# Holding one batch's v loads and moving their casts in a fused linear-attention and MLP kernel

## The chip, the cores and the metric

The kernel runs on one core of a Trainium2 chip. The metric is the device time of one launch in microseconds (us); lower is better. A core has TensorE (PE in the profile, its weight loads PEld), VectorE (DVE), ScalarE (ACT), GpSimd (POOL) and SyncE (SP), each with an instruction stream of its own that is executed in order, and 16 DMA engines, which the queues of SP, ACT and POOL share.

## The reference

Inputs q, k, v are [8 batches, 8 heads, 576 tokens, 64]; the MLP has a gain of 512, w_ch1 of 512x2048 and w_ch2 of 2048x512, all float32. The inputs that matter are computed so:

```python
q_s = exp(q - max(q, -1));  q_s /= sum(q_s, -1) + 1e-9
k_s = exp(k - max(k, 2));   k_s /= sum(k_s, 2) + 1e-9
kv  = einsum('bhsd,bhse->bhde', k_s, v)
att = einsum('bhsd,bhde->bhse', q_s, kv)
x   = att.transpose(0, 2, 1, 3).reshape(8, 576, 512)
xn  = (x - mean(x)) / sqrt(var(x) + 1e-6) * g_ln
out = x + relu(xn @ w_ch1) @ w_ch2
```

## The kernel before, in words

**Chunks.** The MLP runs over nine chunks of 512 tokens. Chunks 0 to 7 are the first 512 tokens of batches 0 to 7, in four blocks t = 0..3 of 128; chunk 8 is the 64 remaining tokens of all eight batches. Chunk c's MLP runs on TensorE while the attention of batch c+1 (and the softmax of batch c+2) is woven between its matmuls. From the second half of chunk 1's first product on, both products are done in seven block products instead of eight, at the price of sums and differences of blocks: sum_x (L244, tile tq, on POOL for most chunks) for the inputs of the first product, sum_h (L561, tile hs, on DVE) for those of the second.

**Order.** Everything stands inside a manual schedule: each engine executes its instructions in the order in which the Python code emits them. run() (L820) walks the list of the main matmul steps of one chunk, adds up their weights, and before each step emits every side step whose position is not above the sum so far. A matmul of the block products weighs 0.5. Chunk 1 has 116 such units: 32 of a plain first product (ph, L505), 28 of the seven-product form (L733, tiles bx, bb, bc), and 56 of the second product (L588, tiles ba, bb, bc, be). Chunks 2 and later have 56 + 56. A position in the diff is thus a place in every engine's stream. Semaphores are derived from the tiles that instructions read and write.

**Buffers.** Tiles come from pools with a fixed number of buffers for each tag, and a new tile takes a buffer when an earlier tile of the tag has been used for the last time. The tag that matters is "ot" of the pool outp, with 4 buffers (L66). It holds the float32 output tiles of 128x512 (y_quarter L594, y_out L518), which are given up when their store to memory is complete, and, for batch 3 alone, the two bf16 halves of v (L145), which are given up when cast_v (L135) has copied them into vm. PSUM tiles "m" have 6 banks (mm_ps, L70); "a" has 2 (att_ps).

**Chunk 1's second product** (mm2_fast L666, lines 706 to 717) allocates four output tiles. Blocks t = 0 and 1 get theirs inside the fifth product (positions 93 and 94.5), where their first column half is written; the second half and the store (L605, issued by POOL) come in the seventh product (about 108.5 and 110). Blocks t = 2 and 3 get theirs in the seventh product (about 111.5 and 113), and have both halves written there.

**Side steps of chunk 1** (second_side, L867) that the change or the prediction speaks of: load_v(3) at 10.1, two loads of v as float32 to bf16 on POOL's queue and two small ones of the remaining tokens (vr, L158); kv_pairs(2) at 40 and the four x_fast(2, t) (L434: a scalar_tensor_tensor from PSUM tile po to x with its sum, L449, and xn, L429); the transposes xn_T(2, 0, 2) at 57.5 and xn_T(2, 2, 2) at 73 by the SP queue (L267); the four sum_x(2, i) on POOL from 95 to 105, which read both transposes; cast_v(3, 0) and cast_v(3, 1) at 101 and 102. POOL therefore has the sums of batch 2 in its stream ahead of all four stores of chunk 1.

**First stage of chunk 2** (attn_fast(3), L851; prep_fast; mm1_fast L736): reduce_q(3, 0, 2) at 4 and reduce_q(3, 2, 2) at 12, their reciprocal at 22, kv_pairs(3) at 24, which reads vm and vr of batch 3, and load_batch(4) at 1, whose loads of q and k are held back by a one-element memset on DVE (L1063). In mm1_fast each pair of groups g, g+1 takes six PSUM banks (x, c, b for each); the product order is 1, 5, 6, 2, 7, 3, 4, and between them stand the ACT copies (L757, L761), the DVE sums add_5 (L764) and out_22 (L767) with its max (L772).

Of the kernel before, what the change touches and what calls it, by code (L numbers as in the profile page):

```python
# [20 lines left out]
def kernel(  # L21
# [16 lines left out]
    nc = tc.nc  # L38
# [66 lines left out]
    def main_src(x, b, h0, hn):  # L105
        return x[b, h0 : h0 + hn, 0:SM, :].rearrange("h (p t) d -> p h (t d)", t=T)
# [28 lines left out]
    def cast_v(b, j):  # L135
        hs = slice(4 * j, 4 * j + 4)
        nc.vector.tensor_copy(
            out=vm[:, b % 2, :, hs, 0:D].rearrange("p t h d -> p h t d"), in_=vts[b][j]
        )

    def load_v(b):

        if b in CAST:
            if b == 3:
                vts[b] = [outp.tile([P, 4, T, D], BF16, tag="ot", name="vt") for _ in range(2)]  # L145
            else:
                vt = mlp.tile([P, H, T, D], BF16, tag=("tq", "hs")[b - 1], name="vt", bufs=1)
                vts[b] = [vt[:, 0:4], vt[:, 4:8]]
            for j, vt in enumerate(vts[b]):
                nc.gpsimd.dma_start(  # L150
                    vt.rearrange("p h t d -> p h (t d)"), main_src(v, b, 4 * j, 4)
                )
        src = v[b, :, 0:SM, :].rearrange("h (p t) d -> p t h d", t=T)
        for t in range(0 if b in CAST else T):
            nc.gpsimd.dma_start(vm[:, b % 2, t, :, 0:D], src[:, t])
        for half in range(2):
            hs = slice(4 * half, 4 * half + 4)
            nc.gpsimd.dma_start(  # L158
                vr[SR * half : SR * half + SR, b % 2, hs, 0:D],
                v[b, hs, SM:S, :].transpose([1, 0, 2]),  # L160
            )
# [54 lines left out]
    def reduce_q(c, t, tn=1):  # L216
        ts = slice(t, t + tn)
        nc.vector.reduce_sum(eqs[c][1][:, ts], eqs[c][0][:, ts], axis=AX.X)  # L218
# [128 lines left out]
    def kv_pairs(b, ts=range(T + 1)):  # L347

        par = b % 2
        if 0 in ts:  # L350
            kvbox["p"] = att_ps.tile([P, NP, P], FP32, tag="a", name="pkv")
        pkv = kvbox["p"]
        for j in range(NP):
            for t in ts:
                for half, ps in enumerate(halves):
                    h = 2 * j + half
                    if t < T:
                        lhsT, rhs = eks[b][:, t, h], vm[:, par, t, h]
                    else:
                        lhsT, rhs = ekr[:, par, h % 4], vr[:, par, h]  # L360
                    nc.tensor.matmul(  # L361
                        pkv[ps, j, 0:VW], lhsT, rhs, start=(t == 0 and j == 0),
                        stop=(t == T), skip_group_check=True,
                    )
        if T in ts:
            rzk = sml.tile([P, NP], FP32, tag="rzk", name="rzk")
            nc.vector.reciprocal(rzk, pkv[:, :, D])
            for half, ps in enumerate(halves):
                nc.vector.tensor_mul(
                    kv_sb[ps, b, :, ps], pkv[ps, :, 0:D], rzk[ps].to_broadcast([64, NP, D])  # L370
                )
# [42 lines left out]
    def square_sum(c, t):  # L414
        x, _, _, mv = xs[c]
        if c:
            nc.scalar.activation(  # L417
                scrap, x[:, t], AF.Square, bias=mv[:, t, 0:1], scale=-float(DM),
                accum_out=mv[:, t, 1:2],
            )  # L420
        else:
            nc.scalar.activation(
                scrap, x[:, t], AF.Square, bias=mv[:, t, 0:1], accum_out=mv[:, t, 1:2]
            )

    def xn_out(c, t):

        x, _, xn, mv = xs[c]
        nc.vector.tensor_scalar(  # L429
            out=xn[:, t], in0=x[:, t], scalar1=float(DM), scalar2=mv[:, t, 0:1],  # L430
            op0=ALU.mult, op1=ALU.subtract,
        )

    def x_fast(c, t):  # L434

        x, st, _, mv = xs[c]
        if c == C9:
            for half in range(2):
                nc.vector.scalar_tensor_tensor(
                    x[:, t].rearrange("p (i two d) -> p i two d", two=2, d=D)[:, :, half],  # L440
                    in0=pobox[c, t][half][:, t % 2], scalar=1.0,
                    in1=eqs[c][2][:, t].rearrange("p (i two) -> p i two", two=2)[:, :, half]
                    .to_broadcast([P, NP, D]),
                    op0=ALU.mult, op1=ALU.mult, accum_out=st[:, t, half : half + 1],
                )
            nc.vector.tensor_add(mv[:, t, 0:1], st[:, t, 0:1], st[:, t, 1:2])
            xn_out(c, t)
            return
        nc.vector.scalar_tensor_tensor(  # L449
            x[:, t].rearrange("p (h d) -> p h d", h=H),  # L450
            in0=pobox[c, t].rearrange("p (h d) -> p h d", h=H), scalar=1.0,
            in1=eqs[c][2][:, t].to_broadcast([P, H, D]), op0=ALU.mult, op1=ALU.mult,
            accum_out=mv[:, t, 0:1] if c else st[:, t, 0:1],
        )
        if c:
            xn_out(c, t)
# [359 lines left out]
    def spread(fns, a, b):  # L816
        n = len(fns)
        return [(a + (b - a) * i / n, fn) for i, fn in enumerate(fns)]
# [29 lines left out]
    def recip_q(c):  # L848
        nc.vector.reciprocal(eqs[c][2], eqs[c][1])

    def attn_fast(c):  # L851

        s = [(4 + 4 * t, lambda t=t: reduce_q(3, t, 2)) for t in (0, 2)] if c == 3 else []
        kv, new, ps, squares, ts, rstd = (
            (24, 40, ((48, 53), (57, 59), (65, 67), (73, 75)), (66, 74, 87, 91), (61, 78), 95)
            if c == 3 else
            (3, 10, ((13, 24), (48, 53), (57, 59), (65, 67)), (60, 66, 74, 87), (55, 70), 92)
        )
        s += [(22 if c == 3 else 2, lambda: recip_q(c)), (kv, lambda: kv_pairs(c)), (new, lambda: start_x(c))]
        for t, (p0, p1) in enumerate(ps):  # L860
            s += spread([lambda t=t, i=i: po_mm(c, t, i) for i in range(NP)], p0, p1)
            s += [(p1, lambda t=t: x_fast(c, t)), (squares[t], lambda t=t: square_sum(c, t))]
        s += [(ts[0], lambda: xn_T(c, 0, 2)), (ts[1], lambda: xn_T(c, 2, 2)), (rstd, lambda: rstd_op(c))]
        s += [((84, 100 if c == C9 - 1 else 88, 92, 101)[i], lambda i=i: sum_x(c, i)) for i in range(4)]
        return s

    def second_side():  # L867

        s = [(p, lambda i=i: quarter_w2(i, 6, 2)) for i, p in enumerate((19, 19.1, 33.9, 66))]
        s += [(6, lambda: xn_pT(1, 3, nc.scalar))]  # L870
        s += [((3, 3.1, 7.5, 7.6)[t], lambda t=t: exp_qt(2, t)) for t in range(T)] + [(7.7, lambda: eq_T(2))]
        s += [(40, lambda: square_sum(1, 2)), (63, lambda: square_sum(1, 3)), (67, lambda: rstd_op(1))]
        s += [(10, lambda: load_batch(3, (2,), eqTs[2][0:1, T - 1, NP - 1, 0:4])), (37, lambda: load_batch(3, (0,)))]
        s += [(p, lambda j=j: cast_v(2, j)) for j, p in enumerate((23, 32.2))]
        s += [(at, lambda i=i: sum_x(1, i)) for i, at in enumerate((9.1, 9.2, 31.5, 36))]
        s += [(10.1, lambda: load_v(3))]
        s += [(101 + j, lambda j=j: cast_v(3, j)) for j in range(2)]
        s += [(9 + 2 * t, lambda t=t: reduce_q(2, t, 2)) for t in (0, 2)]
        s += [(36, lambda: recip_q(2))]
        s += [(18, lambda: exp_k(2, 0, 4)), (28.5, lambda: exp_k(2, 2, 4)), (33, lambda: prep_kvrem(2))]  # L880
        s += [(40, lambda: kv_pairs(2))]
        s += [(40, lambda: start_x(2))]
        for t, (p0, p1) in enumerate(((47, 49), (51, 54), (57, 61), (65, 69))):
            s += spread([lambda t=t, i=i: po_mm(2, t, i) for i in range(NP)], p0, p1)
            s += [(p1, lambda t=t: x_fast(2, t)), ((69, 78, 84, 90)[t], lambda t=t: square_sum(2, t))]
        s += [(57.5, lambda: xn_T(2, 0, 2)), (73, lambda: xn_T(2, 2, 2)), (96, lambda: rstd_op(2))]
        s += [(81, lambda: exp_q(3, 0, 4)), (86, lambda: exp_q(3, 2, 4)), (90, lambda: eq_T(3))]
        s += [(102, lambda: exp_k(3, 0, 4)), (109, lambda: exp_k(3, 2, 4)), (111, lambda: prep_kvrem(3))]
        s += spread([lambda i=i: sum_x(2, i) for i in range(4)], 95, 108)
        return s  # L890
# [283 lines left out]
```

## Time and profile before

| | us |
|---|---|
| Median of 3 runs | 264.73 (264.06 to 266.44) |
| Span of the profiled execution, first to last instruction | 262.9 |
| PE busy in it | 255.6 (97%) |
| DVE busy | 223.4 (85%) |
| ACT busy | 176.8 (67%) |
| POOL busy | 94.2 (36%) |
| TensorE's mean granted clock | 0.998 |

Of the profiled execution the span alone is recorded; the median lies 1.83 us above that span, for what comes before the first and after the last instruction. Times in the views are counted from the start of the span. In a timeline each row is: start, duration, engine, line, operation, output <- input with partitions x elements and type, the count of instructions merged, and in brackets the idle time of the engine ahead of it with what ended it. In a table of stages each row is a stretch, its length, then for PE, PEld, DVE, ACT and POOL the busy time with the count, the granted clock, the mean number of busy DMA transfers per engine, and GB/s.

### The profile page before, as it was taken

To read this page: it belongs to the slowest core of one execution; us is meant where nothing else is said; L and a number is where in the kernel's file an instruction comes from. 1 tells how busy PE (TensorE), PEld (TensorE's weight loads), DVE (VectorE), ACT (ScalarE), POOL (GpSimd) and SP (SyncE) were. 2 spreads that over 40 slices of the span, in tenths; PEclk is the share of its full clock that TensorE was granted. 3 is DMA by queue.
4 is the path that set the end of the run, shared out by engine and by line. 5 is a ranking of instruction groups with operands and counts; after the bars stand their busy time and mean duration, and the time that the engine had idled before them with its cause. 6 is when DMAs were issued, how large, how long until landed. Compare 5 with 4: busy or idle time off the path is not lost.

```text
span 262.9 us, 6770 instructions
## 1 busy us (share of the span) xinstructions
PE 255.6 (97%) x2656; PEld 220.1 (84%) x2659; DVE 223.4 (85%) x504; ACT 176.8 (67%) x348; POOL 94.2 (36%) x148
## 2 busy tenths in 40 slices
PE   8999999999999999999999999999999999999993
PEld 6789755788878998899899988988898888888882
DVE  6768996989998999799889988998898979977872
ACT  4647780997976886689578957894789277537400
POOL 4953228414039404930781088009100800030000
PEclk9999999999999999999999999999999999999999
DMA  6999999998999995899489938994905323221014
GB/s 204 252 202 207 358 215 269 282 188 260 187 151 341 232 119 58 266 278 111 100 251 280 140 82 270 261 167 100 271 11 107 113 102 44 42 110 52 0 41 120
DMA packets 82504, 45.00 MB, mean 171 GB/s; under 512 B 58084, under 2 KB 79080, under 8 KB 82472
## 3 DMA queue, kind: packets, MB, share of 16 engines
q0 software_dynamic: 32464, 21.76, 45.3%
q1 hardware_dynamic: 49424, 22.29, 40.1%
q10 hardware_dynamic: 584, 0.53, 0.6%
q8 instruction: 20, 0.33, 0.5%
q14 instruction: 12, 0.10, 0.1%
HBM read 36.70 MB, written 9.44 MB: 175 GB/s over the span
## 4 chain that ended last, share of the span: by engine, by line
PE 89%; DMA 4%; POOL 2%; DVE 2%; issue 1%; ACT 0%; POOLq 0%
PE ba L588 20%; PE bx L733 19%; PE bb L733 10%; PE ph L505 8%; PE be L588 5%; PE bb L588 5%; PE bc L588 5%; PE pc L541 5%; PE bc L733 5%; DMA w_raw<-in_moe_w_ch_dram 3%; PE po L404 2%; PE pkv L361 2%; DMA qt<-in_q_dram 2%; PE ptr L909 1%; POOL v L987 1%; POOL qt L951 1%
## 5 line engine op out<-in xcount | busy, mean ns | idle before, releaser
L588 PEld LDWEIGHTS <-hs 128*128 128x128 bf16 x512 | 49.8, 98 | 5.7
L733 PEld LDWEIGHTS <-w_raw 128*128 128x128 bf16 x480 | 45.5, 98 | 6.4 <-issue 1.2
L259 POOL TENSOR_TENSOR tq<-xnT 128x256 bf16<-128x256 bf16 x26 | 16.7, 662 | 75.3 <-DMA xnT<-xn 48.7
L588 PEld LDWEIGHTS <-hT 128*128 128x128 bf16 x384 | 37.2, 98 | 4.3
L733 PEld LDWEIGHTS <-w1g 128*128 128x128 bf16 x360 | 34.3, 98 | 4.5 <-issue 0.4
L733 PE MATMUL bx<-tq,w_raw 128*128 128x256 bf16 x240 | 31.6, 273 | 0.2 <-ACT s L761 0.2
L588 PE MATMUL ba<-w_q,hs 128*128 128x256 bf16 x256 | 30.8, 273 | 0.0
L757 ACT COPY bc<-bx 128x512 f32<-128x512 f32 x30 | 16.7, 595 | 19.0 <-PE bx L733 19.0
L764 DVE TENSOR_TENSOR bb<-bx,s 128x512 f32<-128x512 f32 x30 | 19.5, 695 | 9.8 <-ACT s L761 7.0
L605 POOL DMA_DIRECT2D out_dram<-ot x28 | 15.4, 557 | 23.7 <-DVE ot L599 23.6
L775 ACT ACTIVATE hT<-bb 128x512 bf16<-128x512 f32 x30 | 16.3, 595 | 10.8 <-PE bb L733 9.6
L417 ACT ACTIVATE scrap<-x,mv 128x512 bf16<-128x512 bf16 x32 | 23.1, 722 | 0.3
L775 ACT ACTIVATE hT<-bc 128x512 bf16<-128x512 f32 x30 | 16.3, 595 | 9.4 <-PE bc L733 9.4
L572 DVE TENSOR_TENSOR hs<-hT 128x1024 bf16<-128x1024 bf16 x32 | 21.7, 685 | 0.5 <-ACT hT L775 0.5
L404 PE MATMUL po<-kv_sb,eqT 128*128 128x128 bf16 x128 | 22.0, 219 | 0.0
L767 DVE TENSOR_TENSOR hT<-bx,s 128x512 bf16<-128x512 f32 x30 | 19.3, 684 | 3.1 <-PE bx L733 3.1
L449 DVE SCALAR_TENSOR_TENSOR x<-po,rq 128x512 bf16<-128x512 f32 x30 | 20.5, 684 | 0.9 <-PE po L404 0.8
L218 DVE TENSOR_REDUCE zq<-eq 128x16 f32<-128x1024 bf16 (+1 forms) x20 | 20.8, 1051 | 0.6 <-ACT eq L209 0.5
L613 ACT COPY s<-ba 128x512 f32<-128x512 f32 x15 | 8.8, 584 | 14.4 <-PE ba L588 9.8
L775 ACT ACTIVATE hT<-bx 128x512 bf16<-128x512 f32 x30 | 16.5, 604 | 0.9 <-PE bx L733 0.9
L761 ACT COPY s<-bb 128x512 f32<-128x512 f32 x30 | 16.6, 622 | 0.6 <-PE bb L733 0.6
L588 PE MATMUL ba<-w_sb,hT 128*128 128x256 bf16 x128 | 16.6, 272 | 0.0
(155 smaller groups left out, 553.5 us busy)
## 6 DMA issues: line engine op xcount, KB each, us to landing
out_dram<-ot POOLq DMA_DIRECT2D x30, 256.0 KB, 5.8
qt<-in_q_dram SPq DMA_DIRECT2D x5, 1024.0 KB, 6.0
kt<-in_k_dram SPq DMA_DIRECT2D x5, 1024.0 KB, 12.5
qt<-in_q_dram POOLq DMA_DIRECT2D x2, 1024.0 KB, 12.9
kt<-in_k_dram POOLq DMA_DIRECT2D x2, 1024.0 KB, 14.3
vm<-in_v_dram POOLq DMA_DIRECT2D x16, 128.0 KB, 11.5
w_raw<-in_moe_w_ch_dram POOLq DMA_DIRECT2D x3, 512.0 KB, 10.9
w_sb<-in_moe_w_ch_dram POOLq DMA_DIRECT2D x3, 512.0 KB, 16.4
```

Of the source, the lines that this page charges most:

```text
L218: nc.vector.reduce_sum(eqs[c][1][:, ts], eqs[c][0][:, ts], axis=AX.X)
L259: eng.tensor_tensor(out=dst[:, t], in0=x[:, t], in1=y[:, t], op=ALU.subtract)
L404: nc.tensor.matmul(pobox["p"][:, i * P : i * P + P], eqTs[c][:, t, i, :], kv_sb[:, c, i, :], start=True, stop=True,)
L417: nc.scalar.activation(scrap, x[:, t], AF.Square, bias=mv[:, t, 0:1], scale=-float(DM), accum_out=mv[:, t, 1:2],)
L449: nc.vector.scalar_tensor_tensor(x[:, t].rearrange("p (h d) -> p h d", h=H), in0=pobox[c, t].rearrange("p (h d) -> p h d", h=H), scalar=1. ...
L505: nc.tensor.matmul(ph[:, m % 2, at : at + tn], (w1g if c else w1_sb)[:, ko, m * P : (m + 1) * P], xnTs[c][:, t0 : t0 + tn, ko, :], start=( ...
L572: nc.vector.tensor_tensor(out=dst, in0=x, in1=y, op=op)
L588: nc.tensor.matmul(hbox[bank][:, t], lhsT, rhs, start=first and (own or t == 0) and k == 0, stop=k == KH - 1, skip_group_check=True)
L733: nc.tensor.matmul(dst[:, q], lhsT, rhs, start=first and q == 0 and ko == 0, stop=ko == 1, skip_group_check=True)
L764: nc.vector.tensor_tensor(out=at[g, "b"], in0=at[g, "x"], in1=at[g, "s"], op=ALU.add)
L767: nc.vector.tensor_tensor(out=h_out(g, 1, 1), in0=at[g, "x"], in1=at[g, "s"], op=ALU.add)
L775: nc.scalar.activation(h_out(g, odd, half), at[g, name], AF.Relu)
```

## The change

The v loads of batch 3 move from position 10.1 to 69.1 of chunk 1, and the first of them gets a memset of one element on DVE ahead of it, which the load must follow; the loads behind it stand in POOL's order. The two casts move from positions 101 and 102 of chunk 1 to 12 and 14 of chunk 2. There, the second reduction of batch 3's q moves from 12 to 20.6 (the first stays at 4). In chunk 1, x_fast(2, 0) moves from 49 to 52.6, which is behind both out_22 of that stage (emitted with the steps at 49.5 and 51.5).

```diff
-    def load_v(b):
+    def load_v(b, held=False):
 
         if b in CAST:
             if b == 3:
@@ -147,6 +147,8 @@
             for j, vt in enumerate(vts[b]):
+                if held and j == 0:
+                    nc.vector.memset(vt[0:1, 0, 0, 0:1], 0.0)
                 nc.gpsimd.dma_start(
                     vt.rearrange("p h t d -> p h (t d)"), main_src(v, b, 4 * j, 4)
                 )
@@ -850,7 +852,8 @@
     def attn_fast(c):
 
-        s = [(4 + 4 * t, lambda t=t: reduce_q(3, t, 2)) for t in (0, 2)] if c == 3 else []
+        s = [(4 + 8.3 * t, lambda t=t: reduce_q(3, t, 2)) for t in (0, 2)] if c == 3 else []
+        s += [(12 + 2 * j, lambda j=j: cast_v(3, j)) for j in range(2)] if c == 3 else []
@@ -873,8 +876,7 @@
-        s += [(10.1, lambda: load_v(3))]
-        s += [(101 + j, lambda j=j: cast_v(3, j)) for j in range(2)]
+        s += [(69.1, lambda: load_v(3, True))]
@@ -882,7 +884,7 @@
-            s += [(p1, lambda t=t: x_fast(2, t)), ((69, 78, 84, 90)[t], lambda t=t: square_sum(2, t))]
+            s += [(p1 if t else 52.6, lambda t=t: x_fast(2, t)), ((69, 78, 84, 90)[t], lambda t=t: square_sum(2, t))]
```

## The prediction

> **What bounds the kernel now.** I read the page first, then a table of stages around the change, then the timelines of DVE, POOL and PE from 72 to 83 us, then the DMA issues. The page says that TensorE is the bound.
>
> ```profile
> span 262.9 us, 6770 instructions
> PE 255.6 (97%) x2656; PEld 220.1 (84%) x2659; DVE 223.4 (85%) x504; ACT 176.8 (67%) x348; POOL 94.2 (36%) x148
> ```
>
> 7.3 us of the span are not PE work, so no reordering can gain more. The table of stages cuts chunk 1 and the start of chunk 2: plain first product to 56, seven-product part to 64, second product to 76.4, first stage of chunk 2 to 83.
>
> ```profile
> 56.00:64.00 8.00, 7.78 (x108) 6.64 (x107) 7.29 (x18) 6.41 (x13) 2.98 (x5) 1.00 0.69 196
> 64.00:76.40 12.40, 12.40 (x119) 11.09 (x117) 12.02 (x28) 11.13 (x24) 0.00 (x0) 1.00 1.34 190
> 76.40:83.00 6.60, 5.79 (x60) 4.73 (x58) 5.17 (x11) 3.70 (x7) 6.33 (x11) 1.00 0.90 264
> ```
>
> PE loses 0.22 us in the first stretch and 0.81 in the third, nothing in the second, where DVE is nearly full as well (12.02 of 12.40). All that this change could win here is 1.03 us, 0.4% of the time. The timelines of PE, POOL and DVE show where the 0.81 goes and what is queued there.
>
> ```profile
> 76.39 1.04 PE L733 MATMUL bx<-xnT,w1g 128*128 128x256 bf16 x8
> 78.01 1.03 PE L733 MATMUL bb<-tq,w_raw 128*128 128x256 bf16 x8 [0.59 <-POOL tq L259]
> 79.27 1.03 PE L733 MATMUL bx<-tq,w_raw 128*128 128x256 bf16 x8 [0.22 <-ACT s L761]
> ```
>
> ```profile
> 76.67 1.29 POOL L259 TENSOR_TENSOR tq<-xnT 128x256 bf16<-128x256 bf16 x2 [14.05 <-PE ba L588]
> ...
> 80.43 1.29 POOL L259 TENSOR_TENSOR tq<-xnT,tq 128x256 bf16<-128x256 bf16 x2
> 81.66 2.22 POOL L605 DMA_DIRECT2D out_dram<-ot  x4
> ```
>
> ```profile
> 72.42 0.87 DVE L599 SCALAR_TENSOR_TENSOR ot<-bc,rstd,x 128x256 f32<-128x256 f32 x2
> 73.21 0.76 DVE L137 COPY vm<-vt 128x1024 bf16<-128x1024 bf16 x2
> 73.87 0.69 DVE L616 TENSOR_TENSOR bb<-bb,s 128x512 f32<-128x512 f32 x1
> 74.84 0.88 DVE L599 SCALAR_TENSOR_TENSOR ot<-be,rstd,x 128x256 f32<-128x256 f32 x2 [0.27 <-PE be L588]
> 75.64 0.87 DVE L599 SCALAR_TENSOR_TENSOR ot<-bb,rstd,x 128x256 f32<-128x256 f32 x2
> 76.59 0.88 DVE L599 SCALAR_TENSOR_TENSOR ot<-ba,rstd,x 128x256 f32<-128x256 f32 x2
> 77.40 1.21 DVE L218 TENSOR_REDUCE zq<-eq 128x16 f32<-128x1024 bf16 x1
> ...
> 79.95 1.30 DVE L764 TENSOR_TENSOR bb<-bx,s 128x512 f32<-128x512 f32 x2 [1.35 <-ACT s L761]
> ```
>
> To see: POOL idles for 14 us, then makes batch 2's sums, and issues the four stores of chunk 1 only after them, though DVE has had the first two tiles ready since 75.7. The wait is put down to PE, but the transpose issued at 69.5 landed 7.0 us later, at 76.5; that is the releaser. Second, DVE casts v at 73.21, **ahead of** the first write to output blocks 2 and 3 at 75.64. That order is what the change breaks.
>
> **The change, part by part.**
>
> *The casts and the ot buffers (the deciding step).* Tag "ot" has four buffers. When DVE comes to block 2's tile (75.64), two belong to blocks 0 and 1 and, before, the other two are v's, free since the casts at 73.21. In the changed order the casts stand behind that write on DVE itself, so v's two buffers cannot come free first. The only ones that can are block 0's, once its store is complete, then block 1's. DVE stands until then, and all behind it: the four remaining output pieces, reduce_q, the memsets for batch 4's loads, add_5. It is no deadlock: sums and stores on POOL do not need DVE. The restart R is a sum of rows:
> - sums start on POOL at 76.67 now. The transposes lose the v traffic of 59.8 to 71 and get it from 69.7 on. The same transpose took 8.7 us (issued 65.4, under the v, q and k loads), 7.0 (issued 69.5, under their tail) and 3.3 (at 94.5, quiet). With v alone beside it I take 6.5, so 76.2; ends 3.3 and 8.7 give 73.0 and 78.4, but the nearer ends are 75 and 77.5.
> - the sums, 76.67 to 81.66: 4.99 us. They end at 81.2.
> - block 0's store, issue to landing: 6.8 in this stage, with batch 4's q and k loads running. Those loads wait for memsets that are now stuck on DVE, so the store runs alone, as the four after 200 us do (median 3.2; 2.8 in the last chunk). I take 3.5; R = 84.7, from 75 + 5.0 + 2.8 = 82.8 to 77.5 + 5.0 + 6.8 = 89.3.
>
> What PE loses: of six "m" banks, b and a of chunk 1 are held by the stuck pieces. x and c of two groups take the other four, so product 5 cannot begin. Its second group, at 78.45 now (78.01 plus four matmuls), needs bank a, free after four pieces of 0.44 and the 0.55 between two store issues, R + 2.0. Delay: R + 2.0 - 78.45 = 8.25 us, less the 0.22 wait at 79.27, which is then gone (the sums are long done): 8.0. By the ends of R: 6.1 to 12.6.
>
> *PE after standing still for 8 us.* No row shows such a gap in mid-kernel; the nearest is the launch.
>
> ```profile
> 1.06 6.25 PE L838 MATMUL warm<-junk 128*128 128x256 bf16 x34 [1.06 <-DVE bones L971]
> ```
>
> 34 matmuls of a kind that costs 109 ns later (16 in 1.75 us, chain of waits) would be 3.7 us, so 2.5 us were lost to a slow start. Ends: 0 (after the 0.59 us gap at 78.01 nothing is slow) and 2.5. Eight microseconds is nearer to the launch, but part of the slow stretch lies beside DVE, which restarts with its own backlog: 1.3. Sum: 9.3 us. The Trainium skill, "TensorE: Matmul & The Clock Gate", section "What's actually happening", has PE at half clock after an idle window of about 3.4 us and for about 3.4 us of work; by it the term would be 1.7 and the time 274.4 (an estimate from that page). The granted clock shows 1.00 through the launch, so that column does not show it.
>
> *The v loads.* Four POOL instructions of 0.78, 0.78, 0.64 and 0.64 us, from 59.8 to 69.6: POOL is empty there (0.00 x0), free again at 72.5, before the sums. One DVE memset, 0.06 us (L1063 row). The loads now took 10.0 to 11.5 us to land; from 69.7 on that is 80 to 83. Under the standing DVE this is hidden. Without it, v would land about when the casts are due (add_5 ends at 81.2) and vr at about 83, when kv_pairs(3) begins (82.85): up to 0.5 us lost.
>
> *Casts gone from 73.21.* 0.76 us less, but the next piece waits for PE's be at 74.84 anyway: nothing. *Casts in, reduction out of the front* in chunk 2: 0.76 ahead of out_22 in place of 1.21, which comes after the max; the reciprocal still stands before kv_pairs(3)'s outputs are wanted at 88.9: -0.2 to +0.2, I take 0.
>
> *x_fast(2, 0) behind out_22.* Now x and xn (60.83 to 62.11) stand ahead of out_22, and PE waits 0.22 us at 62.76. Moved, out_22 starts when its product is done (about 61.1), and that wait goes. But the third po tile (62.98) has the PSUM buffer that x_fast(2, 0) must read first; two out_22 and the max end at 62.7, x at 63.4, so PE waits 0.4 there. From 63.7 DVE's order and work are the same. 0, between -0.2 and +0.4; and R hangs on batch 2's last x, not on this.
>
> Sum: 8.0 + 1.3 = 9.3. The profiled execution has a span of 262.9 and its own time is not recorded beyond that; 272.2 of span and the same 1.83 that lie outside before give 274.0, against the median 264.73.
>
> **The rivals.**
>
> 1. *No standstill, and so not slower.* Blocks 2 and 3 find buffers in time. For this speaks that the kernel holds two more "ot" tiles than it needs only here, and that I read the buffer rule from the code, as no row before shows such a wait. Against it: four buffers, four tiles in use, and the casts behind the writes. It decides only if block 0's store is complete by 75.6, which the trace excludes as long as POOL has the sums first (81.66). Then only the small terms are left: at best the 1.03 us, at worst 0.5 + 0.4 + 0.2. 264.7, from 263.7 to 265.8.
>
> 2. *The standstill is longer.* The transpose meets the v loads head on (8.7 us, sums from 78.2), the store takes 6.8 as now, and PE restarts as at launch: R = 78.2 + 5.0 + 6.8 = 90.0; 90.0 + 2.0 - 78.45 - 0.22 + 2.5 = 15.8, or 280.6. For it: v's loads and the second transpose are issued within 0.2 us of each other. Against: total traffic is less than at 65.4, and q and k of batch 4 stand still with DVE.
>
> 3. *The hold frees the transpose, and that is all of it.* The first transpose (8.7 us) goes faster; the sums start by 75 and all of the 0.81 is won: 263.9, with rival 1's condition. It is counted within it.
>
> **How the numbers follow.** Forecast, 274.0, its own ends 6.1 and 12.6 + 2.5: chance 0.78. Rival 2: 0.12. Rivals 1 and 3: 0.10. The range 270.0 to 278.5 leaves out the rivals' 0.10 below, most of rival 2 and few of the extreme sums: 2 in 10. A measurement of this kernel tells about 1% (2.6 us) from no change. Faster by more would need over twice the 1.03 us that there is: 0.02. Within 1%: 0.09. Slower: 0.89.
>
> **What would show it.** A DVE piece ot<-bb at about 84 to 86 us with some 9 us of idle ahead of it, ended by the DMA out_dram<-ot; PE idle for 7 to 9 us at product 5 of chunk 2, and slow matmuls right after; reduce_q(3, 0) and batch 4's loads as late as DVE. POOL's sums should stay within 75 to 77.5 and the v loads start at 69.7. From there on each stage should have its old length, shifted. The prediction is wrong if ot<-bb comes at 75.6 with no wait, if PE begins product 5 at 78, or if the sums move to after 78.5 because the transpose is held up.

## The result, and the profile after

| | before | after |
|---|---|---|
| Median of 6 runs, us | 264.71 (264.03 to 266.44) | 273.56 (272.12 to 275.95) |
| Ratio to before, 95% interval | | 1.0356 (1.0321 to 1.0392) |
| Span of the profiled execution, us | 262.9 | 271.3 (its own time 273.22) |

The kernel became 3.6% slower, about 8.9 us; 274.0 us was forecast. One execution further down, the profiled one of e10_five, was a disturbed one (277.18 us, where that kernel's others took 272.75 to 273.76), so only the form of its wait is used. Lines of the kernel stand two higher than before (L601 is the old L599, L735 the old L733). From the page after, the row of PE and of its clock in 40 slices:

```profile
span 271.3 us, 6775 instructions
...
PE   8999999999945999999999999999999999999993
...
PEclk9999999999995999999999999999999999999998
```

One dent, in slices 12 and 13 (75 to 88 us), holds nearly all of the loss; from slice 2 to 39 all else is at 9, as the whole of that stretch is before. Slice 13 also has a lower clock. DVE's timeline there:

```profile
75.11 0.88 DVE L601 SCALAR_TENSOR_TENSOR ot<-be,rstd,x 128x256 f32<-128x256 f32 x2 [0.43 <-PE be L590]
82.99 0.48 DVE L601 SCALAR_TENSOR_TENSOR ot<-bb,rstd,x 128x256 f32<-128x256 f32 x1 [7.01 <-DMA out_dram<-ot]
83.77 0.48 DVE L601 SCALAR_TENSOR_TENSOR ot<-bb,rstd,x 128x256 f32<-128x256 f32 x1 [0.29 <-DMA out_dram<-ot]
...
88.61 1.22 DVE L137 COPY vm<-vt 128x1024 bf16<-128x1024 bf16 x2
```

DVE, whose piece only writes an output tile, waits 7.01 us for a **store**: ot<-bb needs the buffer that block 0's store is still reading. The second wait, 0.29, is block 1's store. The casts that would have freed two buffers stand at 88.61, behind the writes that need them. POOL, which issues the stores:

```profile
70.42 1.56 POOL L152 DMA_DIRECT2D vt<-in_v_dram  x2 [12.82 <-DVE hs L574]
71.95 1.27 POOL L160 DMA_DIRECT2D vr<-in_v_dram  x2
73.20 1.34 POOL L261 TENSOR_TENSOR tq<-xnT 128x256 bf16<-128x256 bf16 x2
...
78.20 1.18 POOL L607 DMA_DIRECT2D out_dram<-ot  x2
84.94 1.07 POOL L607 DMA_DIRECT2D out_dram<-ot  x2 [5.56 <-DVE ot L601]
```

The sums begin at 73.20 with no wait (76.67 before): the transpose of the last blocks, issued at about 69.4, now lands in 3.1 us, by 72.5, where it took 7.0, and POOL is busy with issuing v's loads until 73.2. The DMA views of 69 to 70 us and of 75 to 79 us (source, queue, KB, us from issue to landing):

```profile
xnT<-xn SPq DMA_TRANSPOSE x1, 3.1
```

```profile
out_dram<-ot POOLq DMA_DIRECT2D x2, 256.0 KB, 4.8
eqT<-eq SPq DMA_TRANSPOSE x1, 10.5
```

The four stores have come apart: two at 78.20, two only after DVE's restart. The first two share the DMA engines with a transpose of eq (the exponentials of batch 3's q), issued at 72.14. PE:

```profile
76.65 1.04 PE L735 MATMUL bx<-xnT,w1g 128*128 128x256 bf16 x8
84.31 1.89 PE L735 MATMUL bb<-tq,w_raw 128*128 128x256 bf16 x8 [6.62 <-DVE ot L601]
85.99 1.91 PE L735 MATMUL bx<-tq,w_raw 128*128 128x256 bf16 x8
87.70 1.36 PE L735 MATMUL bc<-xnT,w1g 128*128 128x256 bf16 x8
88.90 1.04 PE L735 MATMUL bx<-tq,w_raw 128*128 128x256 bf16 x8
```

Eight matmuls take 1.04 us before the standstill, 1.9 after it, and 1.04 again from 88.9. The table of stages has the granted clock beside it (the last three numbers of a row are clock, DMA, GB/s):

```profile
77.50:81.50 4.00, 0.19 (x2) 0.00 (x0) 0.00 (x0) 0.85 (x2) 1.88 (x4) 1.00 1.33 141
81.50:84.30 2.80, 0.00 (x0) 0.00 (x0) 1.02 (x3) 0.00 (x0) 0.00 (x0) 0.51 0.44 152
84.30:88.40 4.10, 4.09 (x20) 2.93 (x21) 2.98 (x7) 1.17 (x2) 3.46 (x5) 0.51 0.51 133
88.40:91.50 3.10, 3.10 (x63) 2.63 (x61) 3.06 (x7) 2.17 (x4) 2.42 (x4) 1.00 1.03 342
```

PE stops at 77.5, the clock goes to half some 4 us later, stays there over the restart at 84.3, and is back at about 88.4.

### The profile page after: what moved, and what is told of

Same layout as the page of the kernel before. It is cut to its first block, busy times and chain, and to the rows that moved or that the text cites. A ratio compares the mean times of both kernels' runs of the same rounds, so it can differ in the third digit from the quotient of the medians.

```text
span 271.3 us, 6775 instructions
## 1 busy us (share of the span) xinstructions
PE 258.0 (95%) x2659; PEld 221.1 (82%) x2659; DVE 224.8 (83%) x505; ACT 176.9 (65%) x348; POOL 94.6 (35%) x148
## 4 chain that ended last, share of the span: by engine, by line
PE 85%; DMA 5%; DVE 4%; POOL 2%; issue 1%; SPq 1%; ACT 0%; POOLq 0%; DVEq 0%
PE bx L735 19%; PE ba L590 18%; PE bb L735 10%; PE ph L507 8%; PE pc L543 5%; PE bc L735 5%; PE bb L590 5%; PE bc L590 5%; PE be L590 5%; PE po L406 2%; DMA kt<-in_k_dram 2%; PE pkv L363 2%; DMA out_dram<-ot 2%; POOL tq L261 1%; DMA xnT<-xn 1%; PE ptr L911 1%
## 5 line engine op out<-in xcount | busy, mean ns | idle before, releaser
L735 PEld LDWEIGHTS <-w_raw 128*128 128x128 bf16 x480 | 46.2, 99 | 13.3 <-DVE ot L601 6.9
L261 POOL TENSOR_TENSOR tq<-xnT 128x256 bf16<-128x256 bf16 x26 | 16.9, 672 | 69.4 <-DMA xnT<-xn 69.3
L735 PEld LDWEIGHTS <-w1g 128*128 128x128 bf16 x360 | 34.5, 98 | 4.3
L735 PE MATMUL bx<-tq,w_raw 128*128 128x256 bf16 x240 | 32.6, 277 | 0.1
L777 ACT ACTIVATE hT<-bc 128x512 bf16<-128x512 f32 x30 | 16.3, 594 | 10.1 <-PE bc L735 10.1
L735 PE MATMUL bb<-tq,w_raw 128*128 128x256 bf16 x120 | 16.4, 282 | 6.6 <-DVE ot L601 6.6
```

Source lines behind the costliest of these rows:

```text
L261: eng.tensor_tensor(out=dst[:, t], in0=x[:, t], in1=y[:, t], op=ALU.subtract)
L735: nc.tensor.matmul(dst[:, q], lhsT, rhs, start=first and q == 0 and ko == 0, stop=ko == 1, skip_group_check=True)
L777: nc.scalar.activation(h_out(g, odd, half), at[g, name], AF.Relu)
```

## The experiments

Theory: blocks 2 and 3 of chunk 1 have no "ot" buffer, since the casts moved behind their writes on DVE; DVE waits for the stores of blocks 0 and 1, PE for DVE, and PE then restarts at half clock. Rivals: the hold of the v loads stops DVE, or DVE's new order in chunk 2 does. Each ratio is to the kernel before, on the same chip.

| run | what it is | us | ratio (95%) |
|---|---|---|---|
| e1_six | change, six ot buffers | 265.39 | 1.0034 (1.0013 to 1.0055) |
| e2_casts_only | casts and reduction moved, alone | 272.89 | 1.0331 (1.0276 to 1.0387) |
| e3_x_only | x_fast(2, 0) moved, alone | 264.75 | 1.0006 (0.9980 to 1.0032) |
| e4_hold_only | hold alone | 270.26 | 1.0208 (1.0162 to 1.0255) |
| e5_warm | change, PE busy through the standstill | 271.81 | 1.0281 (1.0243 to 1.0318) |
| e6_six_x49 | e1, x_fast(2, 0) at its old place | 264.66 | 1.0020 (0.9998 to 1.0042) |
| e7_act_store | change, two stores issued by ACT | 274.39 | 1.0375 (1.0334 to 1.0416) |
| e8_six_casts_only | e2, six ot buffers | 264.50 | 1.0011 (0.9989 to 1.0033) |
| e9_act_store_early_v | e2, two stores issued by ACT | 268.87 | 1.0218 (1.0174 to 1.0263) |
| e10_five | change, five ot buffers | 273.35 | 1.0360 (1.0327 to 1.0394) |

**e1_six: the buffers**

```diff
-    outp = ctx.enter_context(tc.tile_pool(name="outp", bufs=4))
+    outp = ctx.enter_context(tc.tile_pool(name="outp", bufs=6))
```

> The changed kernel with six buffers of the tag ot in place of four, all orders kept. Theory (DVE stands still because blocks 2 and 3 of chunk 1 have no buffer until the stores of blocks 0 and 1 are complete): the 7.01 and 0.29 us waits of the pieces ot<-bb are gone, PE begins product 5 of chunk 2 at about 77.5 in place of 84.31, no slow matmuls follow, and the time is 264.2 us, between 263.5 and 265.2. Rival (the held v loads or the moved casts stop DVE by themselves): still over 270.

265.39 us: of 3.6% there are 0.3% left, with every instruction in the changed order. DVE and PE of e1:

```profile
75.99 0.87 DVE L601 SCALAR_TENSOR_TENSOR ot<-bb,rstd,x 128x256 f32<-128x256 f32 x2
...
80.77 1.24 DVE L137 COPY vm<-vt 128x1024 bf16<-128x1024 bf16 x2
```

```profile
77.61 1.04 PE L735 MATMUL bb<-tq,w_raw 128*128 128x256 bf16 x8
...
88.33 1.20 PE L735 MATMUL bx<-tq,w_raw 128*128 128x256 bf16 x8 [0.72 <-DVE bb L766]
```

No wait at ot<-bb, product 5 without a gap, no slow matmuls. That settles the main cause. The time is 0.2 us above the end of my range: in this execution PE waits 0.72 us at 88.33 for a DVE that now has the casts in this stage (e6 and e8, below, come back to that).

**e10_five: one buffer short**

```diff
-    outp = ctx.enter_context(tc.tile_pool(name="outp", bufs=4))
+    outp = ctx.enter_context(tc.tile_pool(name="outp", bufs=5))
```

> The changed kernel with five ot buffers. Theory: block 2's piece finds the fifth buffer at 75.9 and does not wait, block 3's needs block 0's store as block 2's did; DVE stands as long, one store less, and 0.8 us are won of the 9: 272.7 us, between 272 and 273.4. Rival (the wait is shared out over the buffers that are missing): about 269.

273.35 us, no better than the change itself. DVE of e10:

```profile
80.14 0.47 DVE L601 SCALAR_TENSOR_TENSOR ot<-bb,rstd,x 128x256 f32<-128x256 f32 x1
87.23 0.48 DVE L601 SCALAR_TENSOR_TENSOR ot<-bb,rstd,x 128x256 f32<-128x256 f32 x1 [6.62 <-DMA out_dram<-ot]
```

One wait of 6.6 us for a store, at block 3's piece, none at block 2's. A buffer too few costs nearly all that two too few cost. The 0.8 us that I expected from one store less cannot be told from none here.

**e2_casts_only: without the hold**

```diff
-        s += [(69.1, lambda: load_v(3, True))]
+        s += [(10.1, lambda: load_v(3))]
```

(against the changed kernel, and x_fast(2, 0) back at 49)

> Casts and the second reduction moved into chunk 2 as in the changed kernel, but the v loads at their old place without the memset, and x_fast(2, 0) at its old place. Theory (the order of the casts and the buffers, not the hold): DVE stands still here too, and longer than in the changed kernel, because the transpose again meets the v loads and POOL's sums end near 81.7 in place of 78.2; restart at 86.5 to 88, time 276.5 us, between 275.5 and 279. Rival (the hold causes the standstill): no wait at ot<-bb and about 264.7.

The cause is confirmed, the number missed: 272.9 us, not 276.5. The standstill is there without hold and memset, but ends at 82.12, no later than with them. POOL and DVE of e2, and its DMA view of 70 to 74 us:

```profile
74.38 1.29 POOL L261 TENSOR_TENSOR tq<-xnT 128x256 bf16<-128x256 bf16 x2 [12.59 <-DMA xnT<-xn]
...
79.38 1.18 POOL L607 DMA_DIRECT2D out_dram<-ot  x2
```

```profile
82.12 0.48 DVE L601 SCALAR_TENSOR_TENSOR ot<-bb,rstd,x 128x256 f32<-128x256 f32 x1 [6.30 <-DMA out_dram<-ot]
```

```profile
eqT<-eq SPq DMA_TRANSPOSE x1, 5.4
```

The sums begin 1.2 us later than in the changed kernel, as the transpose took 4.6 us and not 3.1, but the store takes 2.7 us from issue to DVE's start (79.38 to 82.12) where it took 4.8 (78.20 to 82.99). The hold takes v's traffic off the transpose of xn, and the store pays. By 78.2 both large loads of v had landed in the changed kernel (5.0 and 7.0 us after their issue), so they are not beside the store themselves; but the transpose of eq, behind them, moved its data only after 76.5 and took 10.5 us in all, into the store. In e2 it took 5.4, was over by 77.4, and nothing else moved beside the store. One of v's small loads was also still under way in the changed kernel; the two were not tried apart.

**e7_act_store and e9_act_store_early_v: stores that do not follow the sums**

```diff
-            nc.gpsimd.dma_start(
+            (nc.scalar if c == FAST and t < 2 else nc.gpsimd).dma_start(
                 out[c, 0:SM, :].rearrange("(p t) n -> p t n", t=T)[:, t], ybox[c, t]
```

(e7: in the changed kernel; e9: in e2)

> The changed kernel with the stores of blocks 0 and 1 of chunk 1 issued by ACT in place of POOL, so that they need not follow batch 2's sums. Theory (DVE waits for the completion of these stores): they are issued near 75.6 in place of 78.2, land 5 to 6.5 us later beside the v loads, DVE restarts at 80.6 to 82, and the time is 271.8 us, between 270.5 and 272.8, with PE still slow after 4 to 5 us of idleness. Rival (the wait ends with something else in POOL's stream): 273.5.

> The kernel of e2 (only casts and reduction moved, v loads early) with the stores of blocks 0 and 1 of chunk 1 issued by ACT. Theory (the early stores of e7 did not land sooner because v's loads were in the way; here v has landed by 72): issued near 76, landing 3 to 4 us later beside the transpose alone, DVE restarts at 79 to 80.5, against 82.12 in e2, and the time is 270.4 us, between 269 and 271.4. Rival (a store issued by ACT is slow by itself): restart near 83, 273 to 274.5.

e7 missed: 274.39, no gain. Its store is issued at 76.49, as soon as block 0's tile is ready, and DVE restarts no sooner. ACT's queue, DVE, and the DMA view of 75 to 79 us in e7:

```profile
76.49 0.38 ACTq L607 DMA_DIRECT2D out_dram<-ot  x1
```

```profile
83.80 0.48 DVE L601 SCALAR_TENSOR_TENSOR ot<-bb,rstd,x 128x256 f32<-128x256 f32 x1 [6.96 <-DMA out_dram<-ot]
```

```profile
out_dram<-ot ACTq DMA_DIRECT2D x2, 256.0 KB, 7.2
eqT<-eq SPq DMA_TRANSPOSE x1, 11.6
```

The wait still ends with that store, but the store takes 7.2 us among the rest of v's loads and a transpose of eq that takes 11.6. In e9, the same stores with v loaded early:

```profile
out_dram<-ot ACTq DMA_DIRECT2D x2, 256.0 KB, 3.2
```

```profile
78.41 0.48 DVE L601 SCALAR_TENSOR_TENSOR ot<-bb,rstd,x 128x256 f32<-128x256 f32 x1 [2.89 <-DMA out_dram<-ot]
```

3.2 us, and 268.87 us in all, better than the 270.4 expected and just below the range. So the standstill ends with the store's completion, and in the changed kernel the held loads cost it time: issuing the store earlier pays only when v is out of the way. In e9's profiled execution PE stood still for 2.5 us and its clock stayed at 1.00:

```profile
79.69 0.61 PE L735 MATMUL bb<-tq,w_raw 128*128 128x256 bf16 x4 [2.46 <-DVE ot L601]
```

**e5_warm: the clock**

```diff
+    def keep_warm(n):
+        w = att_ps.tile([P, 512], FP32, tag="a", name="keep")
+        for _ in range(n):
+            nc.tensor.matmul(w[:, 0:256], junk[:, 0:P], junk, start=True, stop=True)
...
+        s += [(4, lambda: keep_warm(60))] if c == 3 else []
```

> The changed kernel with 60 matmuls of 128x256 on zeros put behind product 1 of chunk 2, into a spare PSUM buffer of the attention; they fill the standstill (6.5 of 6.9 us at 109 ns) and their result is not used. Theory (PE's slow matmuls after the standstill come from its idleness): DVE's restart stays near 83, products 5, 6 and 2 run at 0.87 us per eight again, granted clock 1.00, and some 1.9 us are won: 271.6 us, between 271 and 272.4. Rival (the slow stretch comes from the restart itself, for instance from loads that start then): 273.5 as the changed kernel.

271.81 us, as expected. PE of e5:

```profile
77.51 6.71 PE L846 MATMUL keep<-junk 128*128 128x256 bf16 x60
84.42 0.61 PE L735 MATMUL bb<-tq,w_raw 128*128 128x256 bf16 x4 [0.19 <-DVE ot L601]
85.20 0.60 PE L735 MATMUL bb<-tq,w_raw 128*128 128x256 bf16 x4 [0.17 <-DVE kt L1072]
...
87.38 1.04 PE L735 MATMUL bx<-tq,w_raw 128*128 128x256 bf16 x8
```

DVE's restart (83.14) is as late as in the changed kernel, the slow stretch is gone, and the ratio falls from 1.0356 to 1.0281: 0.0075 of 264.5 is 2.0 us. The two were measured apart, each against the kernel before, and their intervals nearly touch. The rows give the price without them: the first group of product 6 starts 5.91 us after DVE's restart in the changed kernel (88.90 against 82.99) and 4.24 us after it here (87.38 against 83.14), 1.7 us less.

**e3_x_only, e6_six_x49, e8_six_casts_only: what else changed**

```diff
-            s += [(p1, lambda t=t: x_fast(2, t)), ...
+            s += [(p1 if t else 52.6, lambda t=t: x_fast(2, t)), ...
```

> The kernel before with x_fast(2, 0) at 52.6 as its only edit. Theory: PE gains the 0.22 us wait at 62.76, loses about 0.6 at the third po tile, and the 0.3 to 0.4 that is left over is taken up by the wait for POOL's sums at 77.4, which do not move: 264.7 us, between 264.2 and 265.2, with PE at 78.0 for product 5 of chunk 2. Rival (it is carried to the end): 265.1.

> The changed kernel with six ot buffers and x_fast(2, 0) back at 49; the hold, the casts and the reduction stay in their new places. Theory (with the standstill gone, what is left over the kernel before is the 0.4 us more that PE waits for the third po tile and the 0.7 us that it waits at 88.3 for a DVE that now has the casts): 265.0 us, between 264.5 and 265.4. Rival (only the place of x_fast costs): 264.2.

> Six ot buffers, and of the change only the casts and the second reduction in chunk 2; v loads and x_fast(2, 0) at their old places. Theory (the casts filled a gap of DVE in chunk 1 and meet a full DVE in chunk 2): the 0.7 us wait of PE near 88 is there without the hold too, 264.9 us, between 264.4 and 265.5. Rival (it is the hold, whose v traffic slows DVE's casts from 0.76 to 1.24 us): 264.2 with casts of 0.76 us.

e3: no difference, 1.0006. PE's 0.22 us wait for out_22 is gone and a longer one has come, at the third po tile:

```profile
63.21 0.23 PE L404 MATMUL po<-kv_sb,eqT 128*128 128x128 bf16 x1 [0.59 <-DVE x L449]
...
77.42 1.04 PE L733 MATMUL bb<-tq,w_raw 128*128 128x256 bf16 x8
```

I expected PE to wait for POOL's sums at 77.4 still. It does not in this execution: the transpose landed in 4.6 us, not 7.0, in a kernel that does not touch it. It took 4.3 to 4.8 in e2, e8 and e9 too, which all have v's loads at their old place; 7.0 stands in the profile of the kernel before alone. So most of the 0.81 us that I counted in the first stage of chunk 2 was one execution's, and there was less to win than 1.03.

e6 and e8 lie in their ranges, but not for the reason given: their intervals hold 1, e1's overlaps with both, and the 0.72 us wait of e1, which I expected in both, is not in e6's trace and is 0.26 in e8's. In e1 the first cast took 0.91 us, in e6 and e8 each cast 0.41 to 0.44, with v's loads held in e6 as in e1, so the hold alone does not slow it; what does stays open. Neither the casts' place nor that of x_fast can be priced closer than a few tenths of a microsecond. No version tried beats the kernel before.

**e4_hold_only: held loads, casts where they were**

```diff
-        s += [(10.1, lambda: load_v(3))]
+        s += [(69.1, lambda: load_v(3, True))]
```

(and the memset in load_v; nothing else of the change)

> The v loads held as in the changed kernel, but casts, reductions and x_fast(2, 0) at the places of the kernel before. Theory: no wait for a store, since the casts free v's buffers ahead of blocks 2 and 3; but DVE now waits at the casts for v, which lands at 76.4 to 77.5 in place of being there at 73.2. That moves DVE's pieces by 3.5 to 4 us and PE's product 5 by about 2.2: 267 us, between 266 and 268.5. Rival (v's landing is hidden): 264.

270.26 us, 1.8 us above my range. DVE, PE, and the stages of e4:

```profile
75.62 3.25 DVE L137 COPY vm<-vt 128x1024 bf16<-128x1024 bf16 x2 [2.46 <-DMA vt<-in_v_dram]
```

```profile
81.09 0.61 PE L735 MATMUL bb<-tq,w_raw 128*128 128x256 bf16 x4 [3.80 <-DVE ot L601]
```

```profile
81.10:81.70 0.60, 0.60 (x4) 0.39 (x5) 0.60 (x2) 0.00 (x0) 0.23 (x1) 0.94 1.53 220
81.70:85.00 3.30, 3.13 (x15) 2.23 (x15) 2.28 (x6) 1.17 (x2) 3.28 (x5) 0.50 0.99 222
```

The wait for v is there, as the theory has it. But the second half of v landed 6.9 us after its issue, at about 78.1, so the casts ended at 78.9 (the row of the first lasts 2.91 us, for a copy that takes 0.42 before; I read it as a wait that is counted as busy time, which is not shown); and I had not counted the clock: PE stood still for 3.8 us, started at full speed at 81.09, and went to half speed 0.6 us later, for 3.3 us. It also shows why casts and loads had to move together: with the loads held, both orders wait.

## Why the prediction was right

**The deciding step held.** The wait, its place (ot<-bb), its releaser (the store) and PE's block at product 5 were as worked out; e1 and e10 show the buffer rule that I had only read from the code. Three of the signs missed their bounds all the same: the piece came at 82.99 and not at 84 to 86, PE was idle for 6.62 us and not 7 to 9, and the sums began before 75.

**R came out near by two errors against each other, and that is luck.** For R, DVE's restart, 84.7 was forecast, from 82.8 to 89.3, and 82.99 measured.
- The transpose: 6.5 us taken, 3.1 measured, so the sums began at 73.2 and not 76.2 (-3.0). I took v as traffic beside it, but v's first load was issued by POOL only at 70.42 and moved its first data after 72.0, when the transpose had moved nearly all of its own. The near row was the quiet one (3.3 at 94.5), which I had named as an end and set aside.
- The store: 3.5 taken, 4.8 measured (+1.3). I counted the absence of batch 4's loads and let the store run alone, but v's moved loads pushed the transpose of eq onto it; e2, where that is over, has 2.8.

**PE's delay.** R + 2.0 was forecast for product 5's second group; e5 has 85.20 for a restart at 83.14, which is R + 2.06. The terms as written do not give it: four pieces of 0.44 and 0.55 are 2.3, and 1.9 if the first piece runs within the 0.55. In e5's trace the first piece and the wait behind it take 0.73, the other three 0.40 to 0.47 each.

**The clock.** 1.3 forecast between 0 and 2.5; 1.7 by the rows of e5, 2.0 by its time. It was mis-sized because I took DVE's backlog as a cover; the eight-matmul rows show that PE was the slower of the two. And I wrote that the granted clock does not show this: at the launch it does not, but in mid-kernel it does (0.51 from 81.5 to 88.4). The Trainium skill, "TensorE: Matmul & The Clock Gate", section "What's actually happening", has half clock after an idle window of 3.4 us that runs freely, and full clock after a busy one. The trace agrees: half clock for 6.9 us here and 3.3 in e4, two windows and one, and none after e9's 2.5 us of idleness. The 1.7 us that the prediction estimated from that page is also what the rows of e5 give.

**The small terms.** x_fast(2, 0): 0 forecast within -0.2 to +0.4; the waits went from 0.22 to 0.59 and the time by 1.0006 (0.9980 to 1.0032). Casts in chunk 2: 0 within 0.2 forecast; PE waits 0.72 there in e1, 0.26 in e8 and not at all in e6, so the term is not priced. DVE had a gap in chunk 1 where the casts stood, and it is now idle time there (0.80 us ahead of 73.98 in the changed kernel), while in chunk 2 DVE of the kernel before has 0.18 us of idle time between 79.95 and 91.

**The sum.** 82.99 + 2.06 - 78.45 - 0.22 is 6.4. The clock's 1.7 comes on top, and 0.4 at 96.15, the place where e1 has its wait for DVE: up to that place PE is 7.89 us later than in the kernel before (91.50 against 83.61), after it 8.32 us (98.28 against 89.96). That is 8.5, against 8.4 between the spans and 8.85 between the medians. The forecast had 8.0 and 1.3: what R gained by coming early, the clock and the casts' stage gave back in part, and that the total came within half a microsecond is luck too.

**The rivals.** Rival 1 would have needed block 0's store complete by 75.6; it was at 82.99. Rival 2 erred on the transpose, but a store as long as its 6.8 is what e7 then showed (7.2). Rival 3's first half is true: the hold does free the transpose, from 4.3 to 7.0 us with v loaded early to 3.1. Nothing of it can be seen behind the standstill.

## What to carry to other kernels

When a step is moved that reads a tile for the last time, count who asks for that buffer before the new place, on the same engine above all: the engine then waits for whatever frees another buffer, here a store with a queue of its own ahead of it. One buffer short cost as much as two, and more buffers removed it at once. A transfer that is held to clear the way for one neighbour can meet the next one, or push it onto a third, as it did here; ask which that is, and whether anybody waits for it.

## What the runs showed of the hardware

- PE's clock can fall after the matmuls have begun again: in e4 it did so 0.6 us after the restart. The fall came 3.2 us (e2) to 5.4 us (e7) after PE's last matmul. A standstill of 3.8 us was followed by 3.3 us of matmuls at half clock, one of 6.6 us by 4.1, and one of 6.5 us (e7) by 5.6.
- The same DMA depends strongly on its company: the transpose of xn took 3.1 us in the changed kernel and 8.7 at its longest before, a 256 KB store 2.8 us with nothing beside it (e2), 4.8 in the changed kernel and 7.2 in e7, the transpose of eq 5.4 us with v loaded early (e2) and 11.6 behind v's held loads (e7).
